# A fused attention, MLP and mixture-of-experts kernel: table and counts in PSUM tiles of their own, three weighted one-hots in one operation, a matrix's lower halves on VectorE

## The chip, the core and the metric

The kernel runs on one NeuronCore of a Trainium2 chip. The metric is the device time of one execution in microseconds (us). The profiler's engines are PE (TensorE matmuls), PEld (its weight loads), DVE (VectorE), ACT (ScalarE), POOL (GpSimd) and SP (SyncE).

## The reference, cut to what matters

2304 tokens (4 batches of 576, 18 tiles of 128), 8 heads of 64, model width 512, 8 experts, every hidden width 1024:

```python
# random-feature attention, for each batch and head
phi = lambda x: exp(x@omega.T - |x|^2/2 - rowmax) / sqrt(128)
kv, z = phi(k).T @ v, phi(k).sum(tokens)
x = phi(q) @ kv / (phi(q) @ z + 1e-6)            # [2304, 512]
# SoLU MLP
h = x @ w_in                                     # [2304, 1024]
s = h * softmax(h)
x = layernorm(s) * g_ln @ w_out                  # [2304, 512]
# top-1 mixture of 8 experts
e = argmax(x @ w_gate)
out = gate_weight * sigmoid(x @ w_output_gate)[e] * (relu(x @ w1[e]) @ w2[e])
```

## The kernel before

**Products.** Every operand of a float32 product is rounded to float32r (the upper half, names ending in `h`), and the remainder is a float32r number too (the lower half, names ending in `l`). `mm3` (L125 is the matmul in it) runs hi*hi, hi*lo and lo*hi into one PSUM accumulation. So each operand costs two operations on its way: ACT copies the upper half (L116 and others), and `sub` (L113) subtracts it on DVE or POOL to leave the lower half.

**First part, up to L742.** Tiles of 128 tokens pass through projections of k, v and q, sums over tokens (`kv`), the rows of x (`num`, `xr`, L391), their transposes (`xT`, L128), h, SoLU and the second product. `PLAN` writes the order out; a scheduler that estimates times decides the real order of the instructions on each engine within it. In the first 70 us the same engines also decode w_in and w_out from float64 words: DVE's operations `f` at L219 to L228, 128x512 each.

**Routing.** `route_counts(a, z)` takes the tokens of some tiles. It makes the expert one-hots and their counts `cnt`; two matmuls of `cnt` with `tri` and `ones` give `pps`, the counts of the tokens ahead; from them come each token's place, its block column `col` and its place in the block `flo`. For each tile DVE then writes `ea` (128x128, L656) and `er` (three 128x160 one-hots, L659: `row` equal to `col`, times the token's number and the two halves of its weight). `products` multiplies `ea` and `er` into the table `tab`. One PSUM tile of two banks, `tab`, holds both: the table in the first bank, and `scratch()` hands out 16 columns of the second for `pps`. `tab` takes the slot of the tile in which attention's sums `kv` were formed, so it has that tile's form.

**The first expert and the last tiles.** From L742 on PE's instructions keep the order of the program. The first expert's first two blocks are filled with tokens of the first 15 tiles, and its `up` (h = relu(x w1), eight steps f of 12 matmuls with 256 columns) runs while the last tile's tokens are routed. `up` takes a PSUM tile `hp` from a pool of two for each f; ACT writes relu's upper half `hth` (L792), DVE the lower half `htl` (L793), and then the tile is free again. Hooks put other work between the steps: at f = 2 `places()` of tile 17 (the two count matmuls stand ahead of f = 2's own), at f = 4 `hots`, at f = 1 to 4 one quarter each of the split of the first expert's w2 (`split_behind`, which issues it behind step 7 of the `up` before, if there is one). Ahead of `up`, `got` (L830) copies the table to SBUF; `down` begins behind `up` and multiplies tile 17's `er` and `ea` early in its first block, before the next blocks are gathered.

Of the kernel before, what the change touches and what calls it, by code (L numbers as in the profile page):

```python
"""Linear (random-feature) attention, then a SoLU MLP, then a top-1 mixture of experts, on one core.

Every float32 product is carried as three single-pass products of exact halves: an operand is
rounded to float32r (its upper 12 significant bits), the rest of it is a float32r number too, and
hi*hi + hi*lo + lo*hi accumulates in float32.

A row's constant |x|^2/2 in the exponent of the features is taken off again, exactly, by the row's
maximum (max(p - c) = max(p) - c), so p - max(p) is what the exponential sees.

Tokens are sorted by expert on chip: each expert's tokens fill items of 640 slots. As many items as  # L10
there are in any case run straight, the rest under nested branches on their number, so that any split
of the tokens is covered. The first item's expert is chosen, and its first blocks are filled, before the
last tokens are routed.
"""
# [8 lines left out]
F32 = mybir.dt.float32  # L23
# [3 lines left out]
ALU = mybir.AluOpType  # L27
# [4 lines left out]
P = 128  # L32
# [15 lines left out]
# the expert that most tokens of the first TE tiles have goes first; the first TA tiles' tokens fill its first CA blocks  # L48
# [3 lines left out]
# items there are in any case, and at most  # L52
# [3 lines left out]
# blocks of each expert's tokens  # L56
# [5 lines left out]
# the order of the loads, and of the work up to tile NTILE - 4: a letter for what, and the tile  # L62
# [13 lines left out]
# tiles up to these are multiplied as float32  # L76
# [4 lines left out]
def moe_kernel(ctx: ExitStack, tc: tile.TileContext, qT, kT, v, bd, w_in, w_out, wg, g_ln,  # L81
# [18 lines left out]
    # w_in and [g w_out, g w_out wg], later an expert's two matrices: upper and lower halves  # L100
# [19 lines left out]
    def in_turn(ins):  # L120
        """Where the order is fixed, keeps the tensor engine's instructions in it."""
        return tc.keep_in_program_order(ins) if fixed[0] else ins
# [12 lines left out]
    with ExitStack() as ab:  # L135
# [15 lines left out]
        # ---- features' matrix, two heads' copies on the diagonal  # L151
# [13 lines left out]
        # ---- w_in, w_out: float32 of 512 float64 numbers a row at a time, from their lower and upper words, then halves  # L165
# [4 lines left out]
        # room for more of each kind: w_in, w_out, v, tiles of q and k  # L170
# [43 lines left out]
        def assemble(i):  # L214
# [3 lines left out]
            # at least 2^-127 (which becomes 0); exponent's low 7 bits and 20 + 3 of the fraction  # L218
# [5 lines left out]
            # the sign, and the upper bit of the exponent, which both formats set from 2.0 on  # L224
            pin(nc.vector.scalar_tensor_tensor(out=m, in0=hi, scalar=-0x40000000, in1=m, op0=ALU.bitwise_and,
                                               op1=ALU.bitwise_or))
            # round to nearest
# [19 lines left out]
        def gate_columns():  # L247
            """Rows of g w_out wg: with them a tile's logits come with its x2."""
# [15 lines left out]
        def decode(n=1):  # L264
            """The next chunks, in stages behind one another."""
# [12 lines left out]
        # ---- attention  # L278
        # a batch's sums over tokens of feature * [v, 1], for even and odd batches
# [31 lines left out]
        def proj(kind, t):  # L311
            """A tile's products with the features' vectors, [token, head, feature], less each head's maximum, exponentiated."""
# [30 lines left out]
        def k_kv(t, e3):  # L343
            """Adds a tile to its batch's sums."""
# [3 lines left out]
            for b, r0, r1, first, last in segments(t):  # L348
                if first:
                    kv_ps[b] = kvp.tile([P, 2, 512], F32, tag="kv", name=f"kv{b}")  # L350
                for h in range(H):
                    c0 = h % 4 * (D + 1)
                    mm(kv_ps[b][:, h // 4, c0:c0 + D + 1], lhsT=e3[r0:r1, h, :], rhs=va[r0:r1, h, :],
                       start=first and h % 4 == 0, stop=last, skip_group_check=True)
                if last:
                    nc.scalar.copy(out=kvs[:, :, b % 2, :].rearrange("p (a h) n -> p a h n", a=2),
                                   in_=kv_ps.pop(b)[:, :, 0:4 * (D + 1)].rearrange("p a (h n) -> p a h n", h=4))
# [13 lines left out]
        def num(t, qt):  # L371
            """A tile's rows of x: feature * sums of feature * v, over feature * sums of feature."""
# [31 lines left out]
        # ---- SoLU MLP  # L404
# [4 lines left out]
        def b_h(t, between=None):  # L409
            """h; and exp(h - max h), with their sums."""  # L410
# [20 lines left out]
        def b_norm(t, ps, s):  # L431
            """s = h softmax(h) - its mean; and 1 / sqrt(var + 1e-6) for later."""
# [28 lines left out]
        def b_x(t, half):  # L461
            """Half of a tile's x2; with the upper half its products with the gates, too."""
# [13 lines left out]
        def b_x2(t):  # L476
            """A tile's x2."""
# [7 lines left out]
        tab = None  # L485
        taken = [0]

        def scratch():
            """16 columns of the bank beside the table's, in turn."""
            i = taken[0] % 32  # L490
            taken[0] += 1
            return tab[:, 1, 2 * E * i:2 * E * (i + 1)]

        # ---- order
# [43 lines left out]
        # ---- routing: a token's place among its expert's tokens, and tables of the tokens at the places  # L538
# [8 lines left out]
        # a token's number and one more, and upper and lower half of its weight  # L547
# [3 lines left out]
        # 8 - e: of equal logits the first counts  # L551
# [11 lines left out]
        def route(a, z):  # L563
            """Tokens of tiles a to z: places after those before them, weights, and products of their one-hots."""
# [441 lines left out]
```

## Time and profile before

| | before |
|---|---|
| three runs | 671.24, 669.63, 671.86 us; median 671.24 |
| profiled execution | span 669.0 us (no time of its own is listed; the runs lie 0.6 to 2.9 us above this span) |
| PE busy | 633.7 us, 95% of the span |
| DVE busy | 361.8 us, 54% |
| ACT busy | 313.1 us, 47% |
| POOL busy | 211.9 us, 32% |

Each row of the profile's second part cuts the span into 40 slices of 16.7 us. A digit is the busy share in tenths, and 9 stands for 90% or more; the row of PE's clock says which share of full speed was granted. A matmul's busy time is modelled and overlaps its neighbours, so the spacing of starts says more than the duration.

### The profile page before, as it was taken

Reading aid. Unit: us, or ns where it says so; the run is one execution under the profiler, and the core shown is the slowest. Engines: PE = TensorE matmul, PEld = TensorE weight load, DVE = VectorE, ACT = ScalarE, POOL = GpSimd, SP = SyncE. Lnnn points to the kernel's source line nnn. Section 1 sums busy time; section 2 is a strip of 40 time slices with the busy share of each in tenths; the row PEclk is TensorE's granted clock in tenths of the full one; section 3 lists DMA queues with packets and bytes.
Section 4 is the critical chain, followed back from the end, with each engine's and each line's share of the span. In section 5 each row is a group of like instructions: output and inputs, shape, how many; then the busy total and the mean of one; then the engine's idle time right before and its main releaser. Section 6 shows DMA issues by size and latency. Waiting matters only on the chain. (4 is left out here: it accounts for less than half of the span.)

```text
span 669.0 us, 10879 instructions
## 1 busy us (share of the span) xinstructions
PE 633.7 (95%) x4110; PEld 580.1 (87%) x4110; DVE 361.8 (54%) x1026; ACT 313.1 (47%) x747; POOL 211.9 (32%) x168
## 2 busy tenths in 40 slices
PE   7697999999999999999999998589999999999995
PEld 6596898999899999999999998579899889889984
DVE  5779869735356454887467478774522222412200
ACT  6576886756546655445452335322442243324210
POOL 0656454321212211111010115535391355216011
PEclk9897999999999999999999999699999999999998
DMA  8953432021112100000004301028533433010001
GB/s 297 268 169 85 140 109 63 28 70 49 48 32 80 33 17 17 2 16 17 17 17 149 150 33 54 11 64 281 208 103 125 158 116 131 16 48 9 1 33 41
DMA packets 39084, 55.25 MB, mean 83 GB/s; under 512 B 6383, under 2 KB 25327, under 8 KB 39024
## 3 DMA queue, kind: packets, MB, share of 16 engines
q1 hardware_dynamic: 32416, 31.86, 15.3%
q0 software_dynamic: 6464, 22.55, 9.7%
q8 instruction: 34, 0.56, 0.4%
q14 instruction: 26, 0.21, 0.1%
q10 hardware_dynamic: 144, 0.07, 0.0%
HBM read 45.03 MB, written 9.96 MB: 82 GB/s over the span
## 5 line engine op out<-in xcount | busy, mean ns | idle before, releaser
L125 PE MATMUL x<-w2h,lth 128*128 128x256 f32 (+1 forms) x288 | 83.8, 291 | 0.3 <-ACT lth L456 0.3
L125 PE MATMUL x<-w2h,ltl 128*128 128x256 f32 (+1 forms) x288 | 82.3, 286 | 0.5 <-DVE ltl L113 0.5
L125 PE MATMUL x<-w2l,lth 128*128 128x256 f32 (+1 forms) x288 | 82.4, 286 | 0.0
L793 DVE SCALAR_TENSOR_TENSOR htl<-hp,hth 128x320 fp32r<-128x320 f32 (+2 forms) x64 | 31.3, 491 | 89.3 <-ACT hth L792 89.3
L125 PE MATMUL hp<-xtl,w1h 128*128 128x320 f32 (+1 forms) x224 | 70.0, 313 | 0.0
L125 PE MATMUL hp<-xth,w1h 128*128 128x320 f32 (+1 forms) x224 | 70.0, 312 | 0.0
L125 PE MATMUL hp<-xth,w1l 128*128 128x320 f32 (+1 forms) x224 | 70.0, 312 | 0.0
L792 ACT ACTIVATE hth<-hp 128x320 fp32r<-128x320 f32 (+2 forms) x64 | 28.1, 438 | 78.7 <-PE hp L125 78.7
L125 PE MATMUL yp<-w2h,hth 128*128 128x512 f32 x160 | 64.3, 402 | 0.0
L125 PE MATMUL yp<-w2l,hth 128*128 128x512 f32 x160 | 63.2, 395 | 0.0
L125 PE MATMUL yp<-w2h,htl 128*128 128x512 f32 x160 | 63.0, 394 | 0.0
L443 POOL TENSOR_SCALAR s<-s,st 128x1024 f32<-128x1024 f32 x18 | 22.5, 1248 | 115.4 <-DVE st L442 92.5
L427 ACT ACTIVATE s<-h,st 128x512 f32<-128x512 f32 x36 | 24.5, 685 | 73.4 <-DVE st L424 73.4
L125 PE MATMUL h<-w1h,xth 128*128 128x512 f32 x144 | 58.7, 408 | 0.0
L125 PE MATMUL h<-w1h,xtl 128*128 128x512 f32 x144 | 57.3, 398 | 0.0
L125 PE MATMUL h<-w1l,xth 128*128 128x512 f32 x144 | 57.0, 396 | 0.0
L125 PEld LDWEIGHTS x<-w2h,ltl 128*128 128x128 f32 x288 | 54.3, 189 | 0.7 <-DVE ltl L113 0.7
L125 PEld LDWEIGHTS x<-w2h,lth 128*128 128x128 f32 x288 | 54.2, 188 | 0.9 <-ACT lth L456 0.5
L125 PEld LDWEIGHTS x<-w2l,lth 128*128 128x128 f32 x288 | 54.2, 188 | 0.3
L113 DVE TENSOR_TENSOR xtl<-xT,xth 128x512 fp32r<-128x512 f32 x36 | 24.8, 688 | 49.9 <-ACT xth L735 38.2
L815 POOL DMA_INDIRECT out_y<-y,idxs x20 | 21.9, 1096 | 82.8 <-ACT y L814 81.3
L422 DVE TENSOR_REDUCE st<-h 128x1 f32<-128x512 f32 x36 | 24.8, 689 | 41.3 <-PE h L125 41.2
(214 smaller groups left out, 1642.4 us busy)
## 6 DMA issues: line engine op xcount, KB each, us to landing
raw<-in_w POOLq DMA_DIRECT2D x12, 1024.0 KB, 6.0
v<-in_v SPq DMA_DIRECT2D x18, 260.0 KB, 3.1
kr<-in_kT SPq DMA_DIRECT2D x18, 256.0 KB, 4.8
qr<-in_qT SPq DMA_DIRECT2D x18, 256.0 KB, 3.0
x2d<-xo SPq DMA_DIRECT2D x18, 256.0 KB, 2.0
win<-in_w_in SPq DMA_DIRECT2D x8, 512.0 KB, 6.9
wout<-in_w_out SPq DMA_DIRECT2D x8, 512.0 KB, 3.9
raw<-in_w SPq DMA_DIRECT2D x4, 1024.0 KB, 8.9
```

The costliest lines, as they stand in the source:

```text
L113: return eng.tensor_tensor(out=out_, in0=a, in1=hi.bitcast(F32), op=ALU.subtract)
L125: return in_turn(nc.tensor.matmul(ps, **kw))
L422: nc.vector.tensor_reduce(out=st[:, n:n + 1], in_=ps, axis=AX.X, op=ALU.max, negate=True)
L427: nc.scalar.activation(out=s[:, n * 512:(n + 1) * 512], in_=pss[n], func=AF.Exp, bias=st[:, 2:3], accum_out=st[:, 4 + n:5 + n])
L443: nc.gpsimd.tensor_scalar(out=s, in0=s, scalar1=rs, scalar2=nmu, op0=ALU.mult, op1=ALU.add)
L792: act = nc.scalar.activation(out=hi, in_=ps[:, 0:n], func=AF.Relu)
L793: dve = nc.vector.scalar_tensor_tensor(out=lo, in0=ps[:, 0:n], scalar=0.0, in1=hi.bitcast(F32), op0=ALU.max, op1=ALU.subtract)
L815: nc.gpsimd.indirect_dma_start(out=out, out_offset=bass.IndirectOffsetOnAxis(ap=idxs[:, col:col + 1], axis=0), in_=y, in_offset=None, boun ...
```

## The change

It has three parts.

1. The two-bank PSUM tile of `kv` becomes two one-bank tiles `kv0` and `kv1`; the copy of a batch's sums to SBUF becomes two copies of half the heads each (four more ACT instructions over the program). In the same slots `tab` keeps only the table, and a tile of its own, `places`, holds the counts' columns.
2. The three `tensor_scalar` of a tile's `er`, 128x160 each, become one `scalar_tensor_tensor` of 128x480, with `row` and the token's three numbers read as broadcasts: 54 DVE instructions become 18.
3. The lower halves of the first expert's w2 (four subtractions of 128x1024) are issued on DVE and no longer on POOL.

Comments go too, which moves lines: from L344 to L659 a line of before is one further down after; L742 and later keep their numbers.

```diff
@@ k_kv
                 if first:
-                    kv_ps[b] = kvp.tile([P, 2, 512], F32, tag="kv", name=f"kv{b}")
+                    kv_ps[b] = [kvp.tile([P, 512], F32, tag=f"kv{g}", name=f"kv{b}_{g}") for g in range(2)]
                 for h in range(H):
                     c0 = h % 4 * (D + 1)
-                    mm(kv_ps[b][:, h // 4, c0:c0 + D + 1], lhsT=e3[r0:r1, h, :], rhs=va[r0:r1, h, :],
+                    mm(kv_ps[b][h // 4][:, c0:c0 + D + 1], lhsT=e3[r0:r1, h, :], rhs=va[r0:r1, h, :],
                        start=first and h % 4 == 0, stop=last, skip_group_check=True)
                 if last:
-                    nc.scalar.copy(out=kvs[:, :, b % 2, :].rearrange("p (a h) n -> p a h n", a=2),
-                                   in_=kv_ps.pop(b)[:, :, 0:4 * (D + 1)].rearrange("p a (h n) -> p a h n", h=4))
+                    for g, ps in enumerate(kv_ps.pop(b)):
+                        nc.scalar.copy(out=kvs[:, 4 * g:4 * g + 4, b % 2, :],
+                                       in_=ps[:, 0:4 * (D + 1)].rearrange("p (h n) -> p h n", h=4))
@@ scratch
-            return tab[:, 1, 2 * E * i:2 * E * (i + 1)]
+            return places_ps[:, 2 * E * i:2 * E * (i + 1)]
@@ hots
-                for i in range(3):
-                    V.tensor_scalar(out=er[:, i, :], in0=row, scalar1=col[:, t - a:t - a + 1], scalar2=tsc[:, t, i:i + 1],
-                                    op0=ALU.is_equal, op1=ALU.mult)
+                V.scalar_tensor_tensor(out=er, in0=row.unsqueeze(1).to_broadcast([P, 3, NR]), scalar=col[:, t - a:t - a + 1],
+                                       in1=tsc[:, t, :].unsqueeze(2).to_broadcast([P, 3, NR]), op0=ALU.is_equal, op1=ALU.mult)
@@ products
-                    mm(tab[:, 0, 0:3 * NR], lhsT=ea, rhs=er.rearrange("p i n -> p (i n)"),
+                    mm(tab[:, 0:3 * NR], lhsT=ea, rhs=er.rearrange("p i n -> p (i n)"),
@@ after V17
-                tab = kvp.tile([P, 2, 512], F32, tag="kv", name="tab")
+                tab, places_ps = (kvp.tile([P, 512], F32, tag=f"kv{g}", name=n) for g, n in enumerate(("tab", "places")))
@@ the first expert
     for c in range(4):
-        hooks.setdefault(1 + c, []).append(lambda c=c: split_behind(raw2, w2h, w2l, (c,), range(4)))
+        hooks.setdefault(1 + c, []).append(lambda c=c: split_behind(raw2, w2h, w2l, (c,), ()))
```

DVE before, from the one-hots of tiles 15 and 16 to the first expert's second step f = 1 (`hp0_0` and `hp0_1` are the tiles of f = 0 and 1; a name's last number is the allocation's own):

```order
L659 TENSOR_SCALAR er15_4912<-row_136,col_15_4886,tsc_138 128x160 x3
L659 TENSOR_SCALAR er16_4918<-row_136,col_15_4886,tsc_138 128x160 x3
L647 RECIPROCAL eo_17_5041<-eo_17_5041 128x1
L830 COPY got_4973<-tab_2834 128x480
L648 TENSOR_TENSOR gw_17_5036<-gw_17_5036,eo_17_5041 128x1
L793 SCALAR_TENSOR_TENSOR htl_0_4972<-hp0_0_0_4975,hth_0_4971 128x256
L650 CAST gwh_17_5047<-gw_17_5036 128x1
L651 COPY tsc_138<-gwh_17_5047 128x1
L652 TENSOR_TENSOR tsc_138<-gw_17_5036,gwh_17_5047 128x1
L608 COPY base_17_5012<-tab_2834 128x16
L793 SCALAR_TENSOR_TENSOR htl_0_4972<-hp0_1_0_4990,hth_0_4971 128x256
```

The same place of DVE after, a little further on, to the fourth step's `htl`:

```order
L659 SCALAR_TENSOR_TENSOR er15_4891<-row_136,col_15_4865,tsc_138 128x480
L659 SCALAR_TENSOR_TENSOR er16_4895<-row_136,col_15_4865,tsc_138 128x480
...
L830 COPY got_4948<-tab_2842 128x480
...
L793 SCALAR_TENSOR_TENSOR htl_0_4947<-hp0_0_0_4950,hth_0_4946 128x256
L609 COPY base_17_4987<-places_2843 128x16
...
L113 TENSOR_TENSOR w2l_74<-raw2_4263,w2h_73 128x2x512
L617 TENSOR_TENSOR seen_17_4985<-seen_17_4985,base_17_4987 128x8
L793 SCALAR_TENSOR_TENSOR htl_0_4947<-hp0_1_0_4965,hth_0_4946 128x256
L113 TENSOR_TENSOR w2l_74<-raw2_4263,w2h_73 128x2x512
L618 TENSOR_TENSOR seen_17_4985<-seen_17_4985,oh_17_4904 128x8
L793 SCALAR_TENSOR_TENSOR htl_0_4947<-hp0_2_0_4982,hth_0_4946 128x256
L113 TENSOR_TENSOR w2l_74<-raw2_4263,w2h_73 128x2x512
L620 TENSOR_REDUCE place_17_4994<-seen_17_4985 128x1
L793 SCALAR_TENSOR_TENSOR htl_0_4947<-hp0_3_0_5046,hth_0_4946 128x256
```

Six `er` have become two, the counts are read from `places`, and `got` and the first `htl` keep their place behind the two `er`. Four `w2l` of 128x1024 have come onto DVE, one between each pair of `htl` from the first to the fifth. Behind them, in an order that has not changed, stand tile 17's place, `ea` and `er` and the last `htl`.

In the first part the scheduler gives another order too. DVE before, about the decoding of w_in's and w_out's chunks 7 to 9 and the first tile's rows `xr0` (second half, from `num0_4`):

```order
L389 TENSOR_SCALAR rd0_4_0_485<-num0_4_480 128x4
L228 TENSOR_SCALAR win7_209<-win7_209 128x512
L219 TENSOR_SCALAR f8_520<-f8_520 128x512
L390 RECIPROCAL rd0_4_0_485<-rd0_4_0_485 128x4
L219 TENSOR_SCALAR f9_530<-f9_530 128x512
L220 TENSOR_SCALAR f8_520<-f8_520 128x512
L391 TENSOR_TENSOR xr0_470<-num0_4_480,rd0_4_0_485 128x256
```

And DVE after at that place:

```order
L390 TENSOR_SCALAR rd0_4_0_488<-num0_4_483 128x4
L225 SCALAR_TENSOR_TENSOR f7_414<-win7_210,f7_414 128x512
L391 RECIPROCAL rd0_4_0_488<-rd0_4_0_488 128x4
L228 TENSOR_SCALAR win7_210<-win7_210 128x512
L219 TENSOR_SCALAR f8_523<-f8_523 128x512
L392 TENSOR_TENSOR xr0_473<-num0_4_483,rd0_4_0_488 128x256
L220 TENSOR_SCALAR f8_523<-f8_523 128x512
```

`xr0`'s second half stands ahead of `f9`'s L219 and `f8`'s L220 after, and behind both before. Its first half, too, comes some rows earlier.

## Rows read from the trace of the kernel before

**Rows 1.** The page's 40 slices: PE's busy tenths and its granted clock.

```profile
PE   7697999999999999999999998589999999999995
PEclk9897999999999999999999999699999999999998
```

**Rows 2.** PE's waits: engine, line, awaited; us in total, times, longest.

```profile
PE tab L125 <- DVE got L830: 7.2, 1, 7.2
...
PE hp L125 <- DVE htl L793: 1.2, 1, 1.2
```

**Rows 3.** PE's timeline about the first expert: start, us, instruction, [idle before, releaser].

```profile
417.43 0.28 PE L125 MATMUL hp<-xtel,w1h 128*128 128x256 f32 x1
417.55 0.28 PE L125 MATMUL hp<-xteh,w1l 128*128 128x256 f32 x1
425.01 0.60 PE L125 MATMUL tab<-cnt,tri 128*128 128x8 f32 x2 [7.19 <-DVE got L830]
...
425.89 0.56 PE L125 MATMUL hp<-xteh,w1h 128*128 128x256 f32 x1
426.25 0.41 PE L125 MATMUL hp<-xtel,w1h 128*128 128x256 f32 x1
426.46 0.41 PE L125 MATMUL hp<-xteh,w1l 128*128 128x256 f32 x1
...
438.88 0.40 PE L125 MATMUL yp<-w2h,hth 128*128 128x512 f32 x1
```

**Rows 4.** DVE's timeline in the same stretch.

```profile
417.06 0.15 DVE L586 TENSOR_REDUCE cnt<-oh 128x8 f32<-128x8 f32 x1
418.47 5.86 DVE L659 TENSOR_SCALAR er<-row,col,tsc 128x160 fp32r<-128x160 f32 x6
...
424.33 0.63 DVE L830 COPY got<-tab 128x480 f32<-128x480 f32 x1
424.95 0.41 DVE L793 SCALAR_TENSOR_TENSOR htl<-hp,hth 128x256 fp32r<-128x256 f32 x1
```

**Rows 5.** POOL's timeline in the same stretch.

```profile
419.30 4.66 POOL L113 TENSOR_TENSOR w2l<-raw,w2h 128x1024 fp32r<-128x1024 f32 x2 [3.33 <-ACT w2h L116]
```

**Rows 6.** DVE's groups by form: busy us, mean ns of one; idle before.

```profile
L793 DVE SCALAR_TENSOR_TENSOR htl<-hp,hth 128x384 fp32r<-128x384 f32 x8 | 4.5, 558 | 11.3 <-ACT hth L792 11.3
...
L793 DVE SCALAR_TENSOR_TENSOR htl<-hp,hth 128x256 fp32r<-128x256 f32 x8 | 3.3, 418 | 5.7 <-ACT hth L792 5.7
...
L906 DVE TENSOR_TENSOR take<-got,which 128x480 f32<-128x480 f32 x3 | 3.1, 1041 | 0.0
```

**Rows 7.** DVE's timeline at earlier `er` and at the first expert's `w1l`.

```profile
391.70 2.54 DVE L659 TENSOR_SCALAR er<-row,col,tsc 128x160 fp32r<-128x160 f32 x9
...
409.10 1.22 DVE L113 TENSOR_TENSOR w1l<-raw,w1h 128x1024 fp32r<-128x1024 f32 x1
410.98 2.70 DVE L113 TENSOR_TENSOR w1l<-raw,w1h 128x1024 fp32r<-128x1024 f32 x1 [0.67 <-ACT w1h L116]
```

**Rows 8.** Windows: us, PE busy (instructions), granted clock, DMA share, GB/s.

```profile
430.00:431.00 1.00, 1.00 (x7) 0.50 0.00 0
431.00:432.00 1.00, 1.00 (x6) 0.71 0.00 0
...
58.00:60.00 2.00, 1.03 (x8) 0.88 0.32 112
64.00:66.00 2.00, 2.00 (x11) 0.50 0.00 0
```

**Rows 9.** DVE's timeline in the first part.

```profile
55.76 1.42 DVE L219 TENSOR_SCALAR f<-f 128x512 f32<-128x512 f32 x1
57.10 1.49 DVE L220 TENSOR_SCALAR f<-f 128x512 int32<-128x512 int32 x1
```

**Rows 10.** PE's timeline at the same place.

```profile
58.97 0.44 PE L128 MATMUL xT<-ident,xr 128*128 128x128 f32 x2 [2.30 <-DVE xr L391]
```

**Rows 11.** A window of 20 us: us, busy of PE, PEld, DVE, ACT, POOL; clock, DMA, GB/s.

```profile
40.00:60.00 20.00, 16.44 (x126) 15.22 (x124) 19.54 (x30) 13.12 (x33) 14.11 (x10) 0.99 0.39 107
```

More of the change, by code (lines that the diff above doesn't have):

```diff
@@ L483, in b_out @@
             nc.sync.dma_start(out=x2d[t * P:(t + 1) * P], in_=xo_t[t])
-        tab = None
+        tab, places_ps = None, None
         taken = [0]
@@ L739, in moe_kernel @@
         load_expert(raw2, w2, meta[0:1, 0:1])
-        table = tab[:, 0, 0:3 * NR].rearrange("p (i n) -> p i n", i=3)
+        table = tab[:, 0:3 * NR].rearrange("p (i n) -> p i n", i=3)
         fixed[0] = True
```

## The prediction

> **What bounds the kernel now.** I read first the page's slices [rows 1]: PE's digit is 9 almost everywhere, so time saved on another engine beside a full PE is worth nothing, and what can be won lies where the digit falls: the first four slices (0 to 67 us) and slices 25 to 27 (401 to 452 us), where PE's clock falls to 6 too. Next, PE's list of waits [rows 2]: its longest single one is 7.2 us, the counts' matmul into `tab` that waits for DVE's `got`. The timeline of PE and of DVE there [rows 3, 4] tells why. PE issues the last matmul of f = 1 at 417.55; the counts are reduced on DVE by 417.21, so the operands of the matmul have long been there. But `places` shares a tile with the table, and DVE reads the table with `got` at 424.33 to 424.96, so PE's write waits until 425.01. `got` itself stands on DVE behind six `er` that take 5.86 us. f = 2 starts at 425.89, the first `down` matmul at 438.88. In between PE also runs at half speed: the granted clock is 0.50 at 430 to 431 us and rises in the microsecond after, to a mean of 0.71 [rows 8], which puts the rise at about 431.6.
>
> The first part is another case: from 40 to 60 us DVE is busy 19.54 of 20 us [rows 11], and PE's transposes of `xr` wait 2.30 us for it [rows 10].
>
> **Separate tiles for table and counts.** The counts' matmul no longer waits for `got` and can run at about 417.9. That alone doesn't free f = 2: its tile `hp` is the one of f = 0, which is free only after `htl` of f = 0, and that still stands on DVE behind `er15`, `er16` and `got` in the order after. So the wait does not go; it becomes a wait for that `htl`, and what it costs is set by how fast DVE gets there.
>
> **One operation for three one-hots.** The six `er` took 5.86 us, 0.98 each, while POOL ran two `w2l` at 419.30 to 423.96 [rows 5]. Nine `er` elsewhere took 2.54 us, 0.28 each [rows 7]. So most of the 5.86 us is not `er`'s work but what it suffers beside POOL, and part 3 takes POOL's work away. The fused 128x480 operation isn't in the trace. Its kind on 128x256 takes 418 ns and on 128x384 558 ns [rows 6]: 1.09 ns a column, hence 0.66 us for 480. That is the lower bound and three undisturbed singles, 0.85, lie near it; the upper one is `take`, a two-input operation on as many columns, 1.04 us [rows 6]. I take 0.66, as the instruction is the same one; at 1.04 the two cost 0.76 us more.
>
> Here a rule speaks against the change. The Trainium skill (VectorE: DVE Perf Modes, "The perf-mode tier table") says that a one-source `tensor_scalar` on float32 in SBUF has a mode of twice the rate, which a two-source operation has not. By its rate the fused operation would take as long as three singles' data at half speed; the rows agree in part, with 0.28 for 160 columns against 0.66 by slope for 480, where fixed costs eat the difference. By the singles undisturbed the two tiles cost 1.69 us, by the fused ones 1.32: a loss or a gain of under half a microsecond, so the fusion itself decides nothing.
>
> **When f = 2 starts.** 418.47 + 2 x 0.66 = 419.8; the small operations between, about 0.2; `got` 0.63; `htl` 0.41 [rows 4]: 421.0 in place of 425.89, a gain of 4.9 us. With 1.04 each it is 421.8.
>
> **The lower halves of w2 on DVE.** Four subtractions of 128x1024 come onto DVE, one between each pair of `htl`. The nearest rows are `w1l`, the same operation: 1.22 us and, beside POOL, 2.70 us [rows 7]. POOL has nothing else there after, so I take 1.22. From f = 1 to f = 4 DVE then needs about 1.22 + 0.41 + two or three small ones = 2.0 us a step. PE's step is 12 matmuls: 0.12 us apart at full clock (417.43, 417.55) that is 1.42, and 0.21 apart at half clock (426.25, 426.46) 2.56 [rows 3]. So at full clock DVE sets the pace until f = 6, whose tile waits for `htl` of f = 4; that is at 421.0 + 4 x 2.0 = 429.0, and two steps more give `down` at 431.9. If PE falls to half clock in its wait of 3.2 us, as it did before, and stays there for 6.6 us after PE resumes, as before (425.0 to 431.6) [rows 3, 8], it makes 2.6 steps at 2.56 and 3.4 at 1.42: 421.0 + 6.6 + 4.85 = 432.4. I take this one, because a gap of only 2.30 us was followed by a fall to half clock too: 0.88 in the window that holds it, 0.50 at 64 to 66 us [rows 8, 10]. `down` starts at 432.4 in place of 438.88: **-6.4 us**. The wait of 1.2 us for `htl` behind `er17` [rows 2] goes with it, since `er17` falls from 3.41 us to one operation; it is ready at about 431, before `down` needs its product. The bounds: -4.9, if all of f = 2 to 7 takes its 12.99 us as before; -7.4 with full clock and DVE's smallest operations overlapping.
>
> The Trainium skill (SBUF — State Buffer, "Who interferes with whom") holds that DVE and POOL lock one another out of ports they share. The trace agrees: 0.98 against 0.28 for `er`, 2.70 against 1.22 for `w1l`. By that rule moving POOL's four operations costs DVE less than their POOL time; the sum above needs only the rows.
>
> **The first part.** Attention's `kv` gets two copies on ACT instead of one, 4 more instructions in all. I cost them at nothing, since ACT is busy only 13.12 of 20 us there [rows 11]; uncovered they would be at most four times a copy of nearly that size, `got`'s 0.63 [rows 4], spread over four batches. But the scheduler answers with another order, of some loads too, whose number stays. `xr0`'s second half no longer stands behind L219 (55.76, 1.42 us) and L220 (57.10, 1.49) of two chunks [rows 9], so the transposes' wait of 2.30 us [rows 10] can go: **-2.3 us**. It is not safe: what is put behind comes later, on an engine that is 98% busy. Bounds: 0, if the postponed decoding is then what PE waits for; -6, if the half clock after this wait (about 59.5 to 66.4, half of which is lost) goes as well, 2.3 + 3.5. What is won stays won, since PE has no digit under 9 from slice 5 to 24 [rows 1].
>
> **The sum.** -6.4 - 2.3 = -8.7. The profiled span would be 660.3. The runs' median lies 2.2 us above the profiled span of 669.0, so 671.24 - 8.7 = **662.5**.
>
> **Rivals.** 0.3% of the time, 2.0 us, is about what a measurement of this kernel can tell from no change.
>
> A. As above, 662.5. Chance 0.48.
>
> B. The first part gains nothing, since DVE's total work there stays what it was: only -6.4, **664.8**. For it: 19.54 us of 20. Chance 0.21.
>
> C. The first part gains its half clock too: 671.24 - 6.4 - 5.8 = **659.0**. For it: half clock followed a wait. Chance 0.12.
>
> D. PE keeps its full clock through the shorter wait at the first expert: 431.5 instead of 432.4, **661.6**. The Trainium skill (TensorE: Matmul & The Clock Gate, "What's actually happening") says the clock falls only after an idle stretch; the gap of 2.30 us followed by 0.50 speaks against counting on that here. Chance 0.07.
>
> E. DVE becomes the bound at the first expert: `w2l` at 2.70 a piece, a step 3.4 us, `htl` of f = 4 at 421.6 + 13.6 = 435.2, `down` at 438.0: -0.9, or with the first part unchanged **670.3**, the same. Against it: POOL is idle there after. Chance 0.07.
>
> F. Slower: the first part's new order leaves PE waiting more often, and its clock at half throughout. PE was busy 16.44 us at 40 to 60 us, nearly all at full clock [rows 11]; at half clock for most of that about 11 us more, so 671.24 - 6.4 + 11 = **675.8**. It decides from 8.4 us of loss on. For it only that DVE is full and its queue has been changed; against it that `xr` comes earlier. Chance 0.05.
>
> **How the numbers follow.** A is the likeliest and gives 662.5. A to D all lie below 669.2: faster 0.88. E is the same, 0.07; F slower, 0.05. The range from 657.5 to 667.5 takes in A to D with the bounds of the fused operation (+0.8), of `down`'s start (-1.0 to +1.5) and of the first part; it leaves out E and F and the ends, about 0.18.
>
> **What would show it.** In PE's waits the 7.2 us for `got` is gone, and one of about 3 us for `htl` stands at `hp`. The fused `er` takes 0.6 to 0.7 us (over 1.0: the rate was wrong). `w2l` on DVE takes about 1.2 (2.7: case E). From PE's end of f = 1 to `down`'s first matmul it is 14.6 us instead of 21.1. In the first part the wait for `xr` near 59 us is under a microsecond, and `h`'s first tile comes some 2 us sooner. The prediction is wrong if the order of DVE after lets something else, a count or `got`, come late at that place, or if the stretch to 70 us becomes longer instead of shorter.

## The result

The changed kernel takes 665.63 us (median of 4 runs, 664.82 to 667.31) against 671.42 us (median of 4) before: ratio 0.9919, 95% interval 0.9900 to 0.9938, or 5.8 us less. The forecast was 662.5 us with a range of 657.5 to 667.5. The profiled execution has a span of 664.3 us, 4.7 less than before; its time was 665.94.

In the page, PE and its clock by slices. The one slice of the clock at 6 is gone, and PE has no slice below 8 at the first expert, where it had an 8, a 5 and an 8 [rows 1]; the last slice is emptier. (`...` marks rows left out, here and below.)

```profile
PE   7597999999999999999999999899999999999994
...
PEclk9898999999999999999999999999999999999997
```

PE's waits after (engine, line, awaited; us in total, times, longest):

```profile
PE kps L322 <- DMA kr<-in_kT: 10.2, 3, 4.4
PE hp L125 <- DVE htl L793: 3.2, 2, 2.9
PE xT L128 <- DVE xr L392: 1.8, 3, 0.7
```

The 7.2 us for `got` [rows 2] has become 2.9 us for the first `htl`, and the longest wait for `xr` 0.7 us instead of 2.30 [rows 10]. PE's timeline at the first expert, from the first matmul of f = 0 to the first of `down`:

```profile
416.38 0.28 PE L125 MATMUL hp<-xteh,w1h 128*128 128x256 f32 x1
...
419.13 0.28 PE L125 MATMUL hp<-xteh,w1l 128*128 128x256 f32 x1
419.25 0.28 PE L125 MATMUL places<-cnt,tri 128*128 128x8 f32 x2
...
422.70 0.39 PE L125 MATMUL hp<-xteh,w1h 128*128 128x256 f32 x1 [2.94 <-DVE htl L793]
424.61 0.39 PE L125 MATMUL hp<-xteh,w1h 128*128 128x256 f32 x1 [0.23 <-DVE htl L793]
...
432.20 0.39 PE L125 MATMUL yp<-w2h,hth 128*128 128x512 f32 x1
```

The counts' matmul follows f = 1 at once (419.25). f = 1 ends at 419.41 (419.13 + 0.28), f = 2 starts 3.29 us later (8.06 before: 417.83 to 425.89, [rows 3]), and `down` 9.5 us after that (12.99 before). DVE in the same stretch:

```profile
415.42 2.16 DVE L614 TENSOR_TENSOR total<-total,base 128x8 f32<-128x8 f32 x1
...
420.07 1.35 DVE L659 SCALAR_TENSOR_TENSOR er<-row,col,tsc 128x480 fp32r<-128x480 f32 x2
...
421.60 0.65 DVE L830 COPY got<-tab 128x480 f32<-128x480 f32 x1
...
422.23 0.42 DVE L793 SCALAR_TENSOR_TENSOR htl<-hp,hth 128x256 fp32r<-128x256 f32 x1
...
422.92 1.22 DVE L113 TENSOR_TENSOR w2l<-raw,w2h 128x1024 fp32r<-128x1024 f32 x1
```

Two fused `er` take 1.35 us, 0.68 each, and a `w2l` 1.22. The granted clock stays at full through the wait (windows: us, PE busy, clock, DMA share, GB/s):

```profile
421.00:422.00 1.00, 0.00 (x0) 1.00 0.00 0
422.00:423.00 1.00, 0.30 (x2) 1.00 0.00 0
```

Before, it had fallen to half within the wait:

```profile
423.00:424.00 1.00, 0.00 (x0) 0.50 0.00 0
```

**Where the 4.7 us of the span come from.** From f = 0's first matmul to `down`'s it was 24.10 us before (414.78 to 438.88) and is 15.82: -8.28. From there to the end of POOL's last `out_y` (the instruction that sends a block of the result out): +0.08. Two things go against it. f = 0 itself begins 1.60 us later than before. And from the end of the last `out_y` to the end of the span it is 7.65 us (655.67 + 0.98 to 664.3), where it was 5.75 (663.25 to 669.0): +1.90. The sum is -4.70. The forecast had -6.4 at the first expert, -2.3 in the first part, and nothing at the end.

### The profile page after: what moved, and what is told of

It is laid out like the page before. It is cut to its first block, busy times and chain, and to the rows that moved or that the text cites. A ratio compares the mean times of both kernels' runs of the same rounds, so it can differ in the third digit from the quotient of the medians.

```text
span 664.3 us, 10847 instructions
## 1 busy us (share of the span) xinstructions
PE 630.7 (95%) x4110; PEld 576.1 (87%) x4110; DVE 355.9 (54%) x994; ACT 313.3 (47%) x751; POOL 201.3 (30%) x164
## 5 line engine op out<-in xcount | busy, mean ns | idle before, releaser
L328 ACT ACTIVATE ke<-kps,kmx 128x128 f32<-128x128 f32 x144 | 40.9, 394 | 16.6 <-DVE kmx L326 16.5
```

The lines of the kernel that those rows point to most:

```text
L328: nc.scalar.activation(out=e3[:, h, :], in_=pss[h // 4][:, h % 4, :], func=AF.Exp, bias=nmx[:, h:h + 1])
```

## The experiments

Every kernel was timed against the kernel before on the same chip, and profiled once. What the expectations call the measure, from the end of f = 1 to `down`, is here taken from f = 0's first matmul, which adds about 3.0 us (24.1 for 21.1). "First h" is the first matmul of the first tile's h, "tail" the time from the end of POOL's last `out_y` to the end of the span, "code" the instruction packets on queue q14; all from the profiled execution.

| kernel | ratio (95%) | first h | f = 0 | f = 0 to down | tail | code |
|---|---|---|---|---|---|---|
| before | 1 | 69.05 | 414.78 | 24.10 | 5.75 | 26 |
| changed | 0.9919 (0.9900 to 0.9938) | 68.83 | 416.38 | 15.82 | 7.65 | 27 |
| e1: part 1 | 1.0027 (1.0015 to 1.0040) | 68.95 | 416.58 | 24.66 | 5.57 | 26 |
| e2: part 2 | 0.9921 (0.9898 to 0.9943) | 69.36 | 414.85 | 19.83 | 5.65 | 26 |
| e3: part 3 | 0.9917 (0.9896 to 0.9939) | 69.29 | 414.85 | 17.08 | 7.75 | 27 |
| e4: parts 2, 3 | 0.9909 (0.9890 to 0.9927) | 69.39 | 415.02 | 17.00 | 7.59 | 27 |
| e5: changed, kv whole | 0.9917 (0.9902 to 0.9932) | 69.93 | 415.38 | 15.91 | 7.58 | 27 |
| e6: changed, 4 memsets | 0.9909 (0.9892 to 0.9926) | 67.37 | 414.88 | 15.85 | 5.67 | 26 |
| e7: e5, marks later | 0.9906 (0.9890 to 0.9921) | 70.26 | 415.69 | 14.80 | 7.30 | 27 |
| e8: parts 1, 3 | 0.9951 (0.9934 to 0.9968) | 67.66 | 414.68 | 17.97 | 7.67 | 28 |
| e9: changed again | 0.9912 (0.9897 to 0.9928) | 68.62 | 416.20 | 17.14 | 7.68 | 27 |
| e10: changed, w1l on DVE | 0.9873 (0.9858 to 0.9888) | 69.50 | 416.86 | 15.03 | 5.70 | 26 |
| e11: e7, w1l on DVE | 0.9861 (0.9846 to 0.9877) | 69.54 | 415.56 | 12.98 | 7.79 | 27 |
| e12: parts 1, 2 | 0.9951 (0.9938 to 0.9965) | 67.00 | 414.02 | 20.31 | 5.65 | 26 |

### The parts alone: e1 to e4

The theory was that f = 2 waits for DVE's queue ahead of the first `htl`, and that this queue is long because of what stands beside POOL's `w2l`; the rival, that the shared tile is the wait. Part 1 alone (the `kv`, `tab` and `places` hunks of the change, of which one is shown):

```diff
...
-                tab = kvp.tile([P, 2, 512], F32, tag="kv", name="tab")
+                tab, places_ps = (kvp.tile([P, 512], F32, tag=f"kv{g}", name=n) for g, n in enumerate(("tab", "places")))
...
```

> Part 1 alone on the kernel before (kv and tab in one-bank tiles; three single er; w2l on POOL). Measure: from the end of PE's f = 1 to the first down matmul, 21.1 us before, 13.0 with all three parts. Theory (DVE's queue ahead of the first htl is what f = 2 waits for; er beside POOL's w2l fills it): f = 2 now waits for htl instead of got, at most 1 us sooner, half clock stays, 20 to 21 us; and the first part's new order brings the end of f = 1 about 1.5 us later, so the time is 671 to 673. Rival (the shared tile is the wait, separate tiles are the gain): f = 2 starts 3 us or more sooner, the measure falls under 17 us, time under 668.

Part 2 alone:

```diff
-                for i in range(3):
-                    V.tensor_scalar(out=er[:, i, :], in0=row, scalar1=col[:, t - a:t - a + 1], scalar2=tsc[:, t, i:i + 1],
-                                    op0=ALU.is_equal, op1=ALU.mult)
+                V.scalar_tensor_tensor(out=er, in0=row.unsqueeze(1).to_broadcast([P, 3, NR]), scalar=col[:, t - a:t - a + 1],
+                                       in1=tsc[:, t, :].unsqueeze(2).to_broadcast([P, 3, NR]), op0=ALU.is_equal, op1=ALU.mult)
```

> Part 2 alone (one fused er for each tile; shared tab; w2l on POOL). Theory: the two fused er of tiles 15 and 16 still run beside POOL's w2l and take longer than 0.68 each, 1 to 2.3 us each; the counts' matmul waits for got 1.5 to 4 us less than 7.2; the measure falls to 15 to 19 us; first part as before; time 666 to 670. Rival (fusing is worthless, since three undisturbed singles cost 0.85 against 0.68): time within 1 us of before.

Part 3 alone:

```diff
-        hooks.setdefault(1 + c, []).append(lambda c=c: split_behind(raw2, w2h, w2l, (c,), range(4)))
+        hooks.setdefault(1 + c, []).append(lambda c=c: split_behind(raw2, w2h, w2l, (c,), ()))
```

> Part 3 alone (w2l on DVE; three single er; shared tab). Theory: six er take 1.7 us instead of 5.86 as POOL is idle beside them, the counts' matmul waits for got about 3 us instead of 7.2, PE keeps its full clock, the measure falls to 13 to 14.5 us; the first part keeps the order of before; time 663 to 665.5, level with or below the changed kernel. Rival (the shared tile is the wait): measure above 18 us, time above 668.5.

And parts 2 and 3, both of these edits without part 1:

> Parts 2 and 3 without part 1. Theory: like part 3 alone, 0.3 us less for the fused er; measure 13 to 14 us; first part's order as before; time 663 to 665, at or below the changed kernel's 665.6, since part 1 costs about 1.5 us in the first part and gives at most 1 us at the first expert. Rival (separate tiles are worth what they seem): 1 to 4 us slower than the changed kernel, 667 to 670.

Separate tiles alone are slower, 1.0027: 673.66 us at the median, a little above the expected 671 to 673. The wait that was for `got` is now for `htl`, and as long, and a second one follows behind `er17`. PE's and DVE's timelines of e1:

```profile
427.19 0.58 PE L125 MATMUL hp<-xteh,w1h 128*128 128x256 f32 x1 [7.29 <-DVE htl L794]
437.05 0.39 PE L125 MATMUL hp<-xteh,w1h 128*128 128x256 f32 x1 [2.85 <-DVE htl L794]
```

```profile
420.27 5.84 DVE L660 TENSOR_SCALAR er<-row,col,tsc 128x160 fp32r<-128x160 f32 x6
```

Part 3 alone leaves the tile shared and the six `er` single, and only takes POOL's work away beside them. Here is e3's DVE timeline:

```profile
418.52 1.73 DVE L659 TENSOR_SCALAR er<-row,col,tsc 128x160 fp32r<-128x160 f32 x6
```

So 4.1 us of the 5.86 [rows 4] were the presence of POOL's subtractions. Part 2 alone reaches nearly the same ratio by another way. Its two `er`, expected to be stretched to 1 to 2.3 us each, take 0.68 each: they are over before POOL's first `w2l` has gone far, and then a one-column product meets it. DVE's and POOL's timelines of e2:

```profile
418.55 1.35 DVE L658 SCALAR_TENSOR_TENSOR er<-row,col,tsc 128x480 fp32r<-128x480 f32 x2
...
420.00 2.11 DVE L648 TENSOR_TENSOR gw<-gw,eo 128x1 f32<-128x1 f32 x1
```

```profile
419.37 2.73 POOL L113 TENSOR_TENSOR w2l<-raw,w2h 128x1024 fp32r<-128x1024 f32 x1 [3.33 <-ACT w2h L116]
```

Parts 2 and 3 remove the same wait, so their gains do not add: 0.79%, 0.83%, together 0.91%. The theory of the queue holds and its rival, the shared tile, falls.

The times were missed all the same: e3 and e4 were to reach 663 to 665.5 and 663 to 665 us and have medians of 666.25 and 665.90. The stretch from the end of f = 1 to `down` came out as expected, at 14.1 and 14.0 us, though the clock, which e3 was to keep at full, fell to half in both profiles shortly after PE's wait (of 3.06 and 2.89 us). A window of e4:

```profile
423.00:424.00 1.00, 1.00 (x7) 0.50 0.00 0
```

What had not been foreseen stands in the table's column "tail": the three kernels without POOL's four subtractions (changed, e3, e4) have a tail some 2 us longer than the three with them (before, e1, e2).

### The first part: e5 and e9

e5 keeps `tab` and `places` apart and undoes only the split of `kv`, by which the scheduler's order of the first part is that of before:

```diff
+    kv_ctx = ctx.enter_context(ExitStack())
-    kvp = ctx.enter_context(tc.tile_pool(name="kvp", bufs=1, space=PSUM))
+    kvp = kv_ctx.enter_context(tc.tile_pool(name="kvp", bufs=1, space=PSUM, side="right"))
...
+                kv_ctx.close()
+                kvp = ctx.enter_context(tc.tile_pool(name="tabp", bufs=1, space=PSUM, side="right", reuse_waits="tile"))
                 tab, places_ps = (kvp.tile([P, 512], F32, tag=f"kv{g}", name=n) for g, n in enumerate(("tab", "places")))
```

> The changed kernel with kv as one two-bank tile again (one copy a batch); its pool is closed after the last v tile and tab and places are taken in its place. So the separate table and counts stay and only the split of kv is undone; DVE's and PE's order in the first part is that of before. Theory (it is the order that the split of kv makes the scheduler choose that costs 1.6 us ahead of the first expert): f = 0 starts at 414.8 to 415.0 instead of 416.4, the measure from the end of f = 1 to down stays 13 to 14 us, time 664.0 to 664.5, faster than the changed kernel by 1 to 1.6 us. Rival (the loss comes from the tiles of routing, or lies in the parts' sum): f = 0 at 416.4, time 665.6.

e9 is the changed kernel, unedited:

> The changed kernel again, beside the next three on one chip. Theory (its first part ends where that of before ends, give or take what one execution differs from the next; the 416.4 of its first profile was one such draw): f = 0 anywhere from 414.7 to 416.6, tail 7.6 us, measure 13 to 15 us by whether PE's clock falls in the wait, time 664.8 to 666. Rival (its order in the first part costs 1.6 us): f = 0 at 416.4 again.

e5's 0.9917 is level with the changed kernel's 0.9919 and 0.9912: undoing the split of `kv` brings nothing clear of noise. Its median, 665.17 us, is above the expected 664.0 to 664.5, and f = 0 starts at 415.38, not by 415.0; the theory that the order costs 1.6 us is wrong in this form. The table's seven profiles of either order show what it does. With the order of before (before, e2 to e5, e7, e11) the first h comes at 69.55 us in the mean and f = 0 another 345.4 to 346.0 us later; with the new order (the other seven) at 68.28, and f = 0 another 347.0 to 347.6 us later. So the first tile's h does come sooner, by 1.3 us, and 1.8 us are lost again behind it. e9's own f = 0, 416.20, fits the rival as well as the theory that was written for it; it takes the other profiles to tell them apart. PE's timeline of the changed kernel shows waits that before has not in this place:

```profile
81.92 1.13 PE L322 MATMUL kps<-bdr,kr 128*128 128x256 f32 x4 [0.42 <-DVE s L438]
110.08 0.94 PE L384 MATMUL num<-kv,qt 128*128 128x130 f32 x6 [0.58 <-DVE w2l L113]
111.29 0.39 PE L125 MATMUL qps<-bdh,qh 128*128 128x256 f32 x1 [0.27 <-DVE s L438]
121.21 0.65 PE L252 MATMUL woT<-ident,f 128*128 128x128 f32 x4 [0.38 <-ACT f L116]
```

These make 1.65 us, but before has other waits in their place: from the first h to f = 0, PE is idle for 3.41 us before and 4.06 after. So waits make up only 0.65 us of the difference in the first two profiles; the other 1.17 lie in PE's busy time, at full granted clock in both, and what causes them is not settled. In the means of seven profiles, 1.72 us are lost by the eighth tile's h, some 143 us behind the first, and nothing more behind it (1.76 at f = 0). One execution's first h lies up to 1.3 us from the mean of its order, and about two thirds of the 1.60 us in the first profile are such a draw (the first h of before 0.5 us ahead of its mean, that of the changed kernel 0.55 behind its own). Net, f = 0 comes 0.5 us later with the new order, in the means; the seven profiles with it spread over 2.8 us (414.02 to 416.86), so 0.5 us cannot be told from no difference.

### The end: e6

```diff
+    pad = rt.tile([P, 1], F32, name="pad")
+    for c in range(4):
+        hooks.setdefault(1 + c, []).append(lambda: nc.gpsimd.memset(pad, 0.0))
```

> The changed kernel with four one-column memsets added on POOL, as many instructions as it has lost there. In all three kernels without the four subtractions on POOL the span ends 7.6 to 7.8 us after the end of POOL's last out_y, in the three with them 5.6 to 5.7, and the 27th packet of instructions is fetched only in the former. Theory (it is the length of POOL's program, and with it where its instructions are fetched at the end, that costs the 2 us): the tail is 5.6 us and 26 packets, time 663.5 to 664. Rival (the tail has another cause, in what DVE does): tail 7.6 us, time 665.6.

The tail is 5.67 us and q14 carries 26 packets, as the theory had it. The row of that queue in the profile's page, of the changed kernel and of e6:

```profile
q14 instruction: 27, 0.22, 0.1%
```

```profile
q14 instruction: 26, 0.21, 0.1%
```

In all 14 profiles 26 packets go with a tail of 5.6 to 5.8 us, 27 or 28 with 7.3 to 7.8. So 1.9 us of the changed kernel's first-expert gain are lost at the end, with nothing to do with the work there. The times cannot show them: e6's ratio, 0.9909, is close to 0.9919 and 0.9912, and its median, 664.78 us, is above the expected 663.5 to 664. The length of POOL's program fits all 14 traces. With its sequencer's instructions counted, POOL has 385 to 390 in the six profiles with the short end and 382 to 384 in the eight with the long one. e11 below, with 27 packets, does not speak against it: it has 384, one fewer than e10 with 26. e6 tests this by adding nothing else; how a shorter program comes to a longer end stays open.

### The fused operation and the place of w2l in the changed kernel: e8 and e12

e8 has three single `er` for a tile again, e12 the four `w2l` on POOL again, each by the lines marked - of part 2 or part 3 above.

> The changed kernel with three single er for a tile instead of the fused one. Theory: six undisturbed singles cost 1.7 us against 1.35 for two fused, f = 2 starts 0.3 to 0.5 us later, measure 13.3 to 13.6, time 665.6 to 666.3. Rival (the fused form is what brings the gain): f = 2 more than 1.5 us later, time above 667.

> The changed kernel with the four w2l back on POOL (parts 1 and 2 alone). Theory: in part 2 alone it was a small DVE product of two inputs (gw, 2.11 us) that stood beside POOL's w2l ahead of got; it does so here too, so f = 2 waits 4.5 to 5 us for htl, the clock falls to half, measure 15.5 to 17, tail 5.7; time 666 to 667.5. Rival (with separate tiles and one er the place of w2l no longer matters): measure under 14, time 663.5 to 665.

In e8 the six singles take 1.73 us instead of 1.35, and PE waits 3.12 us instead of 2.94: directly 0.2 to 0.4 us, as the theory had it. But from the end of f = 1 to `down` it is 15.0 us where 13.3 to 13.6 were expected, and the median, 667.24 us, is above the expected 666.3. The ratio is 0.9951, 0.3% above the changed kernel's; its interval does not meet that of e9, and does meet that of the first measurement. The granted clock fell during the wait and stayed at half through f = 2 and 3; windows of e8:

```profile
419.00:420.00 1.00, 0.00 (x0) 0.85 0.00 0
420.00:421.00 1.00, 0.00 (x0) 0.50 0.00 0
...
425.00:426.00 1.00, 1.00 (x6) 0.50 0.00 0
```

In e9, the changed kernel itself, it fell too, later and for less, after PE had resumed at 422.50:

```profile
424.00:425.00 1.00, 0.78 (x5) 0.53 0.00 0
```

So a wait of this length sometimes costs clock. Seven profiles have one of 2.89 to 3.12 us: the clock stayed at full in three (the changed kernel's first, e5, e6) and fell in four (e3, e4, e8, e9). That it does so more often in e8 would explain the 0.3%; one profile each cannot show it.

In e12 the small product meets POOL's `w2l` again, in its DVE timeline, PE waits 4.91 us for `htl`, and then half clock follows:

```profile
419.17 2.12 DVE L649 TENSOR_TENSOR gw<-gw,eo 128x1 f32<-128x1 f32 x1
```

```profile
422.31 0.57 PE L125 MATMUL hp<-xteh,w1h 128*128 128x256 f32 x1 [4.91 <-DVE htl L793]
```

Its median was 668.07 us and from the end of f = 1 to `down` it is 17.3 us, both a little above what was expected (667.5 and 17). The theory of the queue holds in both.

With these two, all eight combinations of the three parts have been timed, and they say something of part 1. Added to before it costs 0.27%, to part 2 0.30% (e12 against e2), to part 3 0.34% (e8 against e3), and to both 0.03 or 0.10% (the changed kernel against e4). The first of these is clear of noise; none is a gain. The fused form beside part 3 is worth 0.08% without part 1 (e4 against e3) and 0.3 to 0.4% with it (the changed kernel against e8). So e8's 0.3% need not belong to the fused form alone.

### What is left of the wait: e7, e10 and e11

e7 takes e5 and moves work behind the first `htl`s (`marks` writes `ea` and `er`, here of tiles 15 and 16; `behind` issues work after the step of `up` that comes before it in the program, as `split_behind` does):

```diff
+            if a == TA:
+                late.append(marks)
+            else:
+                marks()
...
-    hooks = {2: [lambda: last.append(places())], 4: [hots]}
+    hooks = {2: [lambda: behind(late[0]), lambda: last.append(places())], 4: [hots]}
     for c in range(4):
-        hooks.setdefault(1 + c, []).append(lambda c=c: split_behind(raw2, w2h, w2l, (c,), ()))
+        hooks.setdefault(3 + c, []).append(lambda c=c: split_behind(raw2, w2h, w2l, (c,), ()))
```

> As e5, and at the first expert ea and er of tiles 15 and 16 stand on DVE behind htl of f = 1, the four w2l one step each from f = 3 to 6 instead of 1 to 4. Theory (f = 2 waits only for the work that stands on DVE ahead of the first htl): f = 2 starts 1.5 to 1.9 us sooner than in e5, the wait falls to under 1.5 us, PE's clock stays at full; DVE then becomes the limit behind f = 3, so of this 1 to 1.9 us reach down; time 662.3 to 663.5. Rival (DVE's total work up to f = 6 sets down's start): down starts as in e5, time 664 to 664.5.

e10 takes the changed kernel and POOL's last share of the first expert, with six memsets:

```diff
-            split_expert(raw1, w1h, w1l, pooled=(1, 3))
+            split_expert(raw1, w1h, w1l, pooled=())
```

> The changed kernel with the first expert's four w1l all on DVE as well (two were on POOL) and six one-column memsets on POOL, as many instructions as POOL has lost against before. Theory (DVE's queue ahead of the first htl is the wait, and a DVE operation with two inputs from SBUF that meets POOL's stands still: w1l 2.70 for 1.22, total 2.16 for 0.16): both stretches go, two more w1l come, DVE is 1 to 1.5 us earlier at the first htl, f = 2 waits about 1.5 to 2 us instead of 2.9, tail 5.7; time 662 to 663.5. Rival (POOL's half was free help, DVE is only loaded more): wait as long or longer, 664 to 666.

e11 has both edits:

> e7 (kv in one tile, marks and w2l later) with w1l on DVE too and the six memsets. Theory: f = 2 waits less than 1 us, DVE's later work then sets the pace, measure 10.5 to 11.9, tail 5.7; time 661 to 662.5, the fastest here. Rival: DVE's total work sets down's start whatever the order, measure 12 to 13, 662.5 to 664.

In e7 the wait falls to 1.86 us, not under the expected 1.5, and `down` starts 1.1 us earlier after f = 0 than in e5. The time is only 0.6 us less at the medians (664.60 against 665.17, with 662.3 to 663.5 expected): inconclusive by itself. e10 is clearly better than the changed kernel, 0.9873 or 663.41 us, just within the expected 662 to 663.5. Two things are in it: the short tail, by its memsets, and less work ahead of the first `htl`. `w1l` runs unstretched and so does the small `total` behind it, 0.16 us where it was 2.16 beside POOL's `w1l`. e10's DVE and PE:

```profile
411.16 3.49 DVE L113 TENSOR_TENSOR w1l<-raw,w1h 128x1024 fp32r<-128x1024 f32 x3
414.64 1.22 DVE L113 TENSOR_TENSOR w1l<-raw,w1h 128x1024 fp32r<-128x1024 f32 x1
415.92 0.16 DVE L614 TENSOR_TENSOR total<-total,base 128x8 f32<-128x8 f32 x1
```

```profile
421.58 0.39 PE L125 MATMUL hp<-xteh,w1h 128*128 128x256 f32 x1 [1.41 <-DVE htl L793]
```

e11 nearly closes the wait (from the end of f = 1 to `down` 10.0 us, a little under the expected 10.5 to 11.9). It has the lowest median, 662.53 us or 0.9861 of before, though the intervals do not tell it from e10; both are faster than the changed kernel. Its PE timeline:

```profile
419.04 0.39 PE L126 MATMUL hp<-xteh,w1h 128*128 128x256 f32 x1 [0.17 <-DVE htl L803]
...
428.54 0.40 PE L126 MATMUL yp<-w2h,hth 128*128 128x512 f32 x1
```

Its tail is 7.79 us against the 5.7 expected, so the 2 us at the end are still to be had in it. e7 has the long tail too, so e11 against e7 shows by itself what `w1l` on DVE is worth: `down` starts 1.8 us earlier after f = 0, and the time is 2.1 us less at the medians, 0.45% by the ratios.

## Why the prediction came out as it did

**The wait for `got` becomes a wait for the first `htl`, at 3.2 us from f = 1's end instead of 8.1.** Right: 3.29 us. e1 shows that separate tiles alone do nothing for it.

**`er`: most of the 5.86 us is POOL's doing; 0.66 us fused.** Right: 0.68 us, and the same six singles take 1.73 us in e3. The mean of 0.98 each hid how: two of the six were stretched, to 2.47 and 2.37 us, and four were not. That "the fusion itself decides nothing" was right for DVE's time (0.4 us) once POOL is out of the way. Beside POOL it decided much, for another reason than its rate: in e2 the two fused `er` were over before POOL stood in their way, and e2 gained 0.79%. A fused `er` that does meet a `w2l` of POOL is stretched like any other: 2.82 us for `er17` in e12.

By the Trainium skill's rule (VectorE: DVE Perf Modes, "The perf-mode tier table") fusing gives up the mode of twice the rate that a one-source `tensor_scalar` on float32 has. The runs do not show that factor: a single took 0.29 us for 160 columns, three of them 0.86, and the fused form 0.68 for 480, so at this size fusing was still the cheaper.

**`w2l` at 1.22 on DVE, `down` 6.4 us earlier, half clock for 6.6 us.** The price was right, 1.22. The term as a whole was too small: from f = 0 to `down` 8.28 us were won in the first profile, at full clock, and 6.96 in e9, with a fall to half of about 3.4 us where 6.6 were forecast. 8.28 is also more than the bound of 7.4 that the prediction gave for full clock, because its step of 2.0 us for DVE was too long: from the first `htl` to that of f = 4 it took 6.67 us for four steps (422.23 to 428.90). So from f = 2 to `down` it was 9.5 us, against 11.4 in case A and 10.5 in the rival D with the clock kept. D was the nearer one in the first profile, by a draw: in e9 the same kernel had the fall.

**The first part, -2.3 us.** This step failed. The wait of 2.30 us for `xr` did go from its place, but the changed kernel's PE timeline has another for `xr` just ahead of the first h:

```profile
68.64 0.44 PE L128 MATMUL xT<-ident,xr 128*128 128x128 f32 x2 [0.65 <-DVE xr L392]
```

And two waits for `qe` between these places grew from 0.80 to 1.76 us together. The first h came 1.3 us sooner in the means, and 1.8 us were lost again before the first expert: net +0.5 us over 14 profiles, +1.60 in the first one. The times of the eight combinations agree that part 1, with its new order, is no gain. The sentence that cautioned against it, that DVE is 98% busy there, was the better guide; the claim that what is won stays won, because PE has no slice under 9 behind, was the error. Waits of 0.3 to 0.6 us do not show in such a digit. What the rival B forecast, a first part that gains nothing, is what the runs show; its reason was not tested by itself.

**The end.** A step that was missing: +1.90 us, undone in e6's profile by four instructions that do nothing for the result.

So the time lay in the range, near case B's 664.8, by a sum of other terms: -8.3 (or -7.0) for -6.4, +0.5 to +1.6 for -2.3, +1.9 for 0. The mechanism at the first expert was right; that the other errors cancelled so far as to leave the total in the range was luck.

## What to carry to other kernels

Ask what a long operation stands beside, not only what it is: here 4.1 of 5.86 us, and 2 us on an operation of one or eight columns, came from another engine's subtractions. Taking `w2l` off that engine was worth 5.7 us (e3), and `w1l` 2 to 3 us more (e11 against e7); the separate tiles were worth nothing. Removing a data dependency gains only the distance to the next thing that is late in the same queue. Of a gain made early under a scheduler ask where the postponed work comes due, and compare the end of the stretch over several profiles before believing a microsecond of it.

## What the runs showed of the hardware

A DVE operation on one or eight columns, with two inputs in SBUF, took 2.11 and 2.16 us beside POOL's subtraction of 128x1024 (`gw` in e2, `total` in the changed kernel) and 0.15 and 0.16 us alone (`gw` in e3, `total` in e10). What it pays is the rest of the subtraction that it meets: `total` above ended at 417.58, and POOL's subtraction, in the changed kernel's POOL timeline, at 417.56:

```profile
414.15 3.41 POOL L113 TENSOR_TENSOR w1l<-raw,w1h 128x1024 fp32r<-128x1024 f32 x1
```

The single `er` paid in the same way. Of the six before, the fourth ended 0.10 us after POOL's first `w2l` and the fifth 0.10 us after its second; DVE's and POOL's timelines of before, narrowed to one operation each:

```profile
419.30 2.47 DVE L659 TENSOR_SCALAR er<-row,col,tsc 128x160 fp32r<-128x160 f32 x1
```

```profile
419.30 2.36 POOL L113 TENSOR_TENSOR w2l<-raw,w2h 128x1024 fp32r<-128x1024 f32 x1 [3.33 <-ACT w2h L116]
```

Not every DVE operation paid: beside POOL's `w2l` in e12, `got` (0.65 us) and `htl` (0.41), which read PSUM, took what they take alone. The Trainium skill (SBUF — State Buffer, "Who interferes with whom") calls the ports that the two share an exclusive lock; these rows agree. They add that the price follows from what is left of the other engine's operation: 2.0 us at one column and at eight, 1.5 us for `w1l` at 1024 columns (2.70 for 1.22).

The end of the program took 5.6 to 5.8 us or 7.3 to 7.8 us behind the same last work, always with 26 instruction packets on one queue or with 27 and more. Four small instructions on POOL moved one kernel from the long end to the short one, and in all 14 traces the two go with 385 and more instructions of POOL, its sequencer's included, or with 384 and fewer. Why stays open.
